# One written order for all five engines in a fused attention and hardswish kernel

## The chip, the cores and the metric

The kernel runs on one core of a Trainium2 chip. The core has five engines, each with its own in-order instruction queue. PE (TensorE) does matrix products from SBUF into PSUM, DVE (VectorE) and ACT (ScalarE) do elementwise work and read PSUM, POOL (GpSimd) does elementwise work in SBUF, and SP (SyncE) issues most DMA transfers. Engines meet through semaphores: an instruction that waits holds everything behind it on its own queue and nothing on the others. PSUM has eight banks of 128 x 512 float32 words. The metric is the time of one execution on the device in microseconds (us), lower is better; the median of several runs is compared.

## The reference

Eight batches (B) of eight heads (H), 512 local and 32 global tokens, head size 64, all float32. Global queries attend to all 544 keys, local queries to the 32 global keys and to local keys at a distance of at most 32. The heads are put side by side (512 columns) and go through an MLP of width 2048:

```python
s_g = scale * q_g @ concat(k_g, k_l).T          # 32 x 544
out_g = softmax(s_g) @ concat(v_g, v_l)
s_ll = where(abs(i - j) <= 32, scale * q_l @ k_l.T, -1e9)
a_l = softmax(concat(scale * q_l @ k_g.T, s_ll))
out_l = a_l @ concat(v_g, v_l)
x = concat(out_g, out_l)                        # (8*544) x 512
h = x @ w_in                                    # 512 -> 2048
out = (h * clip(h + 3, 0, 6) / 6) @ w_out       # 2048 -> 512
```

## The kernel before

**Units of work.** The 64 heads are taken as 32 pairs, numbered p = 0 to 31; pair p belongs to batch b = p // 4 and is its m = p % 4. For each pair:

- `load` (lines 113 to 125): SP brings k, q and v, 256 KB each, into staging buffers `stg` (13 of them); `cast` (127 to 136) makes them fp16 (`kn`, `qn`, and v into `vt`); `vshift` (138 to 141) copies half of `vt` to `vb`, which holds the values shifted by half a block; `vglob` (143 to 147) puts the global values there; `kglob` (198 to 201) puts the global keys between the local ones.
- `emit_T` (203 to 227) transposes keys and queries. Batches 0 and 1 do it on PE (four 128 x 128 transposes into PSUM, copied out by DVE or ACT); from batch 2 on SP issues one DMA transpose for each. `qwrap` (229 to 231) repeats 32 query columns.
- `emit_S` (233 to 255): the local scores in two halves (ch 0 and 1), for both heads, so 16 matmuls in all; ACT takes the exponential into `E`. The band is applied in one of two ways: either PE first adds a mask (`mneg`, two matmuls of 512 columns for each half, line 242), or DVE multiplies `E` by a 0/1 mask afterwards (`mk`, line 254, two for each half).
- `emit_SG` and `emit_PG` (257 to 314): scores and values of the global queries. `emit_AV` (275 to 299): values of the local queries, 32 matmuls, then DVE's reciprocal and product into `xn`. `emit_X` (316 to 331) transposes `xn` into `xt`, on PE for batches 0 and 1, by DMA from batch 2 on. `emit_XG` (333 to 342) normalises the global rows into `xg`.

The MLP of a batch (`moe_units`, 344 to 380) has a first product (16 column chunks c, each four matmuls over m from `xt`, line 354), ACT's ReLU (359), DVE's gate (361) into `gt`, and a second product (line 370: four output tiles t of 16 matmuls each, in groups of four, c4), whose result is copied out (374) and stored by SP (376). The first product of a batch needs the `xt` of all four of its pairs. After batch 7 the 256 global rows of all batches go through the same MLP as a ninth set (called 8 in the change), with 256 columns in the first product.

**Weights.** 16 + 16 loads of 256 KB (`load_w`) and as many casts (`cast_w`). Global keys and queries come in strips of 64 KB, one for each batch (`load_g`), and are transposed on PE in `emit_G`.

**PSUM.** Seven banks rotate in the pool `psp` (line 52), one tag for all tiles; the eighth holds the global values.

**What sets the order.** The program is written as calls of these functions; the framework's planner then orders each engine's instructions by priorities, dependencies and costs. Where `pin` (94 to 103) is called, it chains every instruction of the named engines to the one traced before it on that engine, without a semaphore, so that the planner keeps the traced order there. Line 608 pins all five engines (`ALL`) for the opening, from the loads to the scores of pair 7 and the first part of batch 1's MLP. For the loop over pairs (610 to 666), which mixes one pair's attention with 8 or so MLP units, and for the end, only SP and POOL (`QUEUES`) are pinned; PE, ACT and DVE are left to the planner. A call such as `emit_S` traces PE's, ACT's and DVE's parts together, and all of a batch's MLP comes in units of a chunk (first product) or of four matmuls (second product). Nearly all casts, shifts and global copies stand on POOL.

Of the kernel before, what the change touches and what calls it, by code (L numbers as in the profile page):

```python
# [14 lines left out]
def kernel(  # L15
# [90 lines left out]
    ALL = (ET.SP, ET.Pool, ET.PE, ET.Activation, ET.DVE)  # L106

    st = {}

    def stage():  # L110
        return wrk.tile([P, 512], FP32, tag="stg", name="stg", bufs=NSTG)

    def load(p, what="kqv"):
        b, m = divmod(p, NM)
        s = st.setdefault(p, {})
        for c in what:
            src = {"k": k_l, "q": q_l, "v": v_l}[c]
            t = stage()
            if c != "v" and b < NRUN:
                nc.sync.dma_start(out=t.rearrange("p (h x) -> p h x", h=2),  # L120
                                  in_=src[b, 2 * m:2 * m + 2].rearrange("h (p j) d -> p h (j d)", j=NT))
            else:
                nc.sync.dma_start(out=t.rearrange("p (h kb d) -> p (h kb) d", h=2, kb=NT),
                                  in_=src[b, 2 * m:2 * m + 2].rearrange("h (kb p) d -> p (h kb) d", p=P))
            s[c + "f"] = t.rearrange("p (h kb d) -> p kb h d", h=2, kb=NT)

    def cast(p, what, eng):
        b, m = divmod(p, NM)
        s = st[p]
        for c in what:  # L130
            if c == "v":
                o = vts[b % NV][:, :, 2 * m:2 * m + 2, 0:D]
            else:
                s[c + "n"] = wrk.tile([P, NT, P], FP16, tag=c + "n", name=c + "n", bufs=4)
                o = s[c + "n"].rearrange("p kb (h d) -> p kb h d", h=2)
            eng.tensor_copy(out=o, in_=s[c + "f"])  # L136
# [15 lines left out]
    w_st = {}  # L152

    def load_w(kind, i):
        t = stage()
        if kind == "in":
            qd, m = divmod(i, NM)
            nc.sync.dma_start(out=t, in_=moe_w_in[m * P:(m + 1) * P, qd * 512:(qd + 1) * 512])
# [43 lines left out]

    def emit_T(p, qdve=False):
        b, m = divmod(p, NM)
        s = st[p]
        kT = kTs[b % 2][:, m]
        kv = kT[:, 0:NT * KW].rearrange("p (u c) -> p u c", u=NT)
        qT = wrk.tile([P, Sl + W], FP16, tag="qT", name="qT", bufs=4)
        s["qT"], s["kT"] = qT, kT
        if b >= NRUN:  # L210
            for c, o in (("k", kv[:, :, 0:P]),
                         ("q", qT[:, W:Sl + W].rearrange("p (u c) -> p u c", u=NT))):
                nc.sync.dma_start_transpose(out=o, in_=s[c + "n"].rearrange("p kb c -> p (kb c)"))
            return
        ps = {}
        for c in "kq":
            ps[c] = ps_tile("psT" + c, FP16)[:, 0:Sl]
            for j in range(NT):
                nc.tensor.matmul(out=ps[c][:, j * P:(j + 1) * P], lhsT=s[c + "n"][:, j], rhs=ident,
                                 is_transpose=True)  # L220
        qcopy = nc.vector.tensor_copy if qdve else nc.scalar.copy
        nc.vector.tensor_copy(
            out=kv[:, :, 0:P].rearrange("p u (i j) -> p u i j", j=NT),
            in_=ps["k"].rearrange("p (j u i) -> p u i j", j=NT, u=NT))
        qcopy(out=qT[:, W:Sl + W].rearrange("p (i j) -> p i j", j=NT),
              in_=ps["q"].rearrange("p (j i) -> p i j", j=NT))
        nc.vector.tensor_copy(out=qT[:, 0:W], in_=qT[:, Sl:Sl + W])

    def qwrap(p):
        qT = st[p]["qT"]  # L230
        nc.gpsimd.tensor_copy(out=qT[:, 0:W], in_=qT[:, Sl:Sl + W])

    def emit_S(p, ch, pe_mask=False):
        s = st[p]
        qT, kT = s["qT"], s["kT"]
        if ch == 0:
            s["E"] = wrk.tile([P, 2, 2, Sl], FP16, tag="E", name="E", bufs=3)
        E = s["E"]
        pss = [ps_tile(f"psS{e}") for e in range(2)]
        if pe_mask:  # L240
            for e in range(2):
                nc.tensor.matmul(out=pss[e], lhsT=ident, rhs=mneg[:, ch], start=True, stop=False,  # L242
                                 skip_group_check=True)
        for w in range(NT):
            c0 = w * KW if ch == 0 else ((w - 1) % NT) * KW + D
            for e in range(2):
                r = slice(e * D, (e + 1) * D)
                nc.tensor.matmul(out=pss[e][:, w * P:(w + 1) * P], lhsT=kT[r, c0:c0 + P],  # L248
                                 rhs=qT[r, w * P:(w + 1) * P], start=not pe_mask, stop=True,
                                 skip_group_check=True)  # L250
        for e in range(2):
            nc.scalar.activation(out=E[:, ch, e], in_=pss[e], func=EXP, scale=qk_scale)  # L252
        for e in range(0 if pe_mask else 2):
            nc.vector.tensor_tensor(out=E[:, ch, e], in0=E[:, ch, e],  # L254
                                    in1=mk[:, ch].rearrange("p w c -> p (w c)"), op=mult)
# [19 lines left out]
    def emit_AV(p):  # L275
        b, m = divmod(p, NM)
        E = st[p]["E"]
        vt, vb = vts[b % NV], vbs[b % NV]
        xn = wrk.tile([P, NT, P], FP16, tag="xn", name="xn", bufs=3)
        st[p]["xn"] = xn  # L280
        for w2 in range(NT // 2):
            po = ps_tile("pav").rearrange("p (w c) -> p w c", w=2)
            for i in range(2):
                w = 2 * w2 + i
                for e in range(2):
                    h = 2 * m + e
                    o = po[:, i, e * DV:e * DV + D + 1]
                    nc.tensor.matmul(out=o, lhsT=E[:, 0, e, w * P:(w + 1) * P],  # L288
                                     rhs=vt[:, w, h, 0:D + 1], start=True, stop=False,
                                     skip_group_check=True)  # L290
                    nc.tensor.matmul(out=o, lhsT=E[:, 1, e, w * P:(w + 1) * P],  # L291
                                     rhs=vb[:, (w - 1) % NT, h, 0:D + 1], start=False, stop=True,
                                     skip_group_check=True)
            pv = po[:, :, 0:2 * DV].rearrange("p w (e c) -> p w e c", e=2)
            rc = wrk.tile([P, 2, 2, 1], FP32, tag="rc", name="rc", bufs=4)
# [223 lines left out]
    for c in range(HEAD, NC):  # L519
        u1(c)  # L520
# [182 lines left out]
```

## Time and profile before

| | us |
|---|---|
| median of 3 runs (328.93 to 331.13) | 329.35 |
| the profiled execution, own time | 329.07 |
| its span, first to last instruction | 327.2 |
| PE busy | 307.9 (94%) |
| DVE busy | 209.3 (64%) |
| ACT busy | 202.5 (62%) |
| POOL busy | 134.3 (41%) |

How to read the rows: the page gives each engine's busy time, then the span in 40 slices whose digit is the busy share in tenths. A group row has line, engine, operation, output and inputs, shapes and count; behind the first bar stand busy time in us and the mean ns of one instruction, behind the second the engine's idle time just before them and what ended it. Instructions overlap in the pipeline, so busy time divided by the count can be less than the mean. A row of the timeline starts with its start and its length in us. "SPq" is SP's queue: the length of an issue there includes what it waited for. PE's ends are modelled, so a busy PE is not always PE at full rate. In rows of DMA issues the last number is the median time from issue to landing.

### The profile page before, as it was taken

Reading aid. Unit: us, or ns where it says so; the run is one execution under the profiler, and the core shown is the slowest. Engines: PE = TensorE matmul, PEld = TensorE weight load, DVE = VectorE, ACT = ScalarE, POOL = GpSimd, SP = SyncE. Lnnn points to the kernel's source line nnn. Section 1 sums busy time; section 2 is a strip of 40 time slices with the busy share of each in tenths; the row PEclk is TensorE's granted clock in tenths of the full one; section 3 lists DMA queues with packets and bytes.
Section 4 is the critical chain, followed back from the end, with each engine's and each line's share of the span. In section 5 each row is a group of like instructions: output and inputs, shape, how many; then the busy total and the mean of one; then the engine's idle time right before and its main releaser. Section 6 shows DMA issues by size and latency. Waiting matters only on the chain.

```text
span 327.2 us, 7442 instructions
## 1 busy us (share of the span) xinstructions
PE 307.9 (94%) x2779; PEld 160.5 (49%) x2779; DVE 209.3 (64%) x469; ACT 202.5 (62%) x401; POOL 134.3 (41%) x240
## 2 busy tenths in 40 slices
PE   7799999999989489999999999999999999999994
PEld 2454446654545245545555455555555555444571
DVE  5377854669967379548955697469745874382260
ACT  8556866688825278448844785468646864481260
POOL 5879868708923834463436244535300000000000
PEclk9799999999999999999999999999999999999998
DMA  8999999999979997999979999799944012101202
GB/s 208 311 374 331 302 259 232 239 193 148 186 150 178 187 221 149 180 211 192 195 116 167 206 163 181 158 198 176 154 107 109 19 21 82 64 0 34 93 5 64
DMA packets 143011, 53.70 MB, mean 164 GB/s; under 512 B 130432, under 2 KB 134528, under 8 KB 142976
## 3 DMA queue, kind: packets, MB, share of 16 engines
q1 hardware_dynamic: 140800, 52.97, 77.8%
q0 software_dynamic: 2176, 0.26, 1.3%
q8 instruction: 22, 0.36, 0.5%
q14 instruction: 13, 0.11, 0.1%
HBM read 35.13 MB, written 8.91 MB: 135 GB/s over the span
## 4 chain that ended last, share of the span: by engine, by line
PE 78%; DVE 9%; DMA 5%; ACT 4%; issue 1%; SPq 1%; POOL 1%; DVEq 0%; ACTq 0%
PE psH L354 33%; PE po L370 31%; PE psS L248 4%; DMA xt<-xn 3%; DVE E L254 3%; ACT E L252 2%; PE pav L291 2%; PE pav L288 2%; DVE gt L361 2%; DMA stg<-in_v_l_dram 2%; PE pg L311 1%; PE psS L242 1%; PE psSG L265 1%; DVE xn L297 1%; ACT t L359 1%
## 5 line engine op out<-in xcount | busy, mean ns | idle before, releaser
L370 PE MATMUL po<-wout,gt 128*128 128x512 f16 x544 | 126.3, 379 | 0.0
L354 PE MATMUL psH<-xt,win 128*128 128x512 f16 x512 | 118.9, 379 | 6.5 <-DMA xt<-xn 5.6
L359 ACT ACTIVATE t<-psH,half_col 128x512 f32<-128x512 f32 (+1 forms) x144 | 91.0, 669 | 25.2 <-PE psH L354 20.0
L361 DVE SCALAR_TENSOR_TENSOR gt<-t,psH 128x512 f16<-128x512 f32 (+1 forms) x144 | 90.4, 653 | 25.2 <-ACT t L359 24.5
L252 ACT ACTIVATE E<-psS 128x512 f16<-128x512 f32 x128 | 66.6, 602 | 46.5 <-PE psS L248 46.4
L354 PEld LDWEIGHTS <-win 128*128 128x128 f16 x576 | 53.5, 98 | 56.0 <-issue 3.3
L370 PEld LDWEIGHTS <-gt 128*128 128x128 f16 x544 | 49.8, 98 | 54.4
L254 DVE TENSOR_TENSOR E<-E,mk 128x512 f16<-128x512 f16 x100 | 51.2, 540 | 9.2 <-ACT E L252 7.2
L136 POOL CAST kn<-stg 128x512 f16<-128x512 f32 x31 | 19.5, 630 | 45.2 <-DMA stg<-in_k_l_dram 44.2
L374 ACT COPY ot<-po 128x512 f32<-128x512 f32 x17 | 10.0, 588 | 36.6 <-PE po L370 36.6
L296 DVE RECIPROCAL rc<-pav 128x4 f32<-128x4 f32 x64 | 10.2, 172 | 29.8 <-PE pav L291 29.7
L374 DVE COPY ot<-po 128x512 f32<-128x512 f32 x17 | 11.7, 690 | 24.6 <-PE po L370 24.6
L297 DVE TENSOR_TENSOR xn<-pav,rc 128x256 f16<-128x256 f32 x64 | 26.2, 422 | 1.4
L136 POOL CAST vt<-stg 128x512 f16<-128x512 f32 x32 | 20.4, 638 | 15.6 <-DMA stg<-in_v_l_dram 13.0
L136 POOL CAST qn<-stg 128x512 f16<-128x512 f32 x32 | 20.8, 651 | 12.8 <-DMA stg<-in_q_l_dram 12.8
L248 PEld LDWEIGHTS <-kT 64*128 64x128 f16 x512 | 14.9, 94 | 18.4 <-issue 16.1
L248 PE MATMUL psS<-qT,kT 64*128 64x128 f16 x512 | 21.8, 219 | 0.7 <-ACT E L252 0.5
L288 PEld LDWEIGHTS <-E 128*128 128x128 f16 x256 | 17.8, 97 | 7.5 <-issue 4.1
L141 POOL COPY vb<-vt 64x512 f16<-64x512 f16 x32 | 20.3, 634 | 2.1
L291 PE MATMUL pav<-vb,E 128*128 128x65 f16 x256 | 20.1, 193 | 0.4 <-DVE E L254 0.3
L288 PE MATMUL pav<-vt,E 128*128 128x65 f16 x256 | 20.2, 192 | 0.1
L291 PEld LDWEIGHTS <-E 128*128 128x128 f16 x256 | 16.8, 97 | 3.9 <-DVE E L254 0.8
(74 smaller groups left out, 223.7 us busy)
## 6 DMA issues: line engine op xcount, KB each, us to landing
stg<-in_k_l_dram SPq DMA_DIRECT2D x32, 256.0 KB, 3.9
stg<-in_q_l_dram SPq DMA_DIRECT2D x32, 256.0 KB, 4.3
stg<-in_v_l_dram SPq DMA_DIRECT2D x32, 256.0 KB, 4.8
out_dram<-ot SPq DMA_DIRECT2D x24, 256.0 KB, 2.2
stg<-in_moe_w_in_dram SPq DMA_DIRECT2D x16, 256.0 KB, 6.3
stg<-in_moe_w_out_dram SPq DMA_DIRECT2D x16, 256.0 KB, 5.6
out_dram<-ot SPq DMA_DIRECT2D x8, 192.0 KB, 2.3
out_dram<-ot SPq DMA_DIRECT2D x16, 64.0 KB, 1.9
```

The costliest lines, as they stand in the source:

```text
L136: eng.tensor_copy(out=o, in_=s[c + "f"])
L248: nc.tensor.matmul(out=pss[e][:, w * P:(w + 1) * P], lhsT=kT[r, c0:c0 + P], rhs=qT[r, w * P:(w + 1) * P], start=not pe_mask, stop=True, sk ...
L252: nc.scalar.activation(out=E[:, ch, e], in_=pss[e], func=EXP, scale=qk_scale)
L254: nc.vector.tensor_tensor(out=E[:, ch, e], in0=E[:, ch, e], in1=mk[:, ch].rearrange("p w c -> p (w c)"), op=mult)
L288: nc.tensor.matmul(out=o, lhsT=E[:, 0, e, w * P:(w + 1) * P], rhs=vt[:, w, h, 0:D + 1], start=True, stop=False, skip_group_check=True)
L291: nc.tensor.matmul(out=o, lhsT=E[:, 1, e, w * P:(w + 1) * P], rhs=vb[:, (w - 1) % NT, h, 0:D + 1], start=False, stop=True, skip_group_chec ...
L297: nc.vector.tensor_tensor(out=xn[:, 2 * w2:2 * w2 + 2].rearrange("p w (e d) -> p w e d", e=2), in0=pv[:, :, :, 0:D], in1=rc.to_broadcast([ ...
L354: nc.tensor.matmul(out=ps[:, 0:n], lhsT=w_in_t[m][:, c * P:(c + 1) * P], rhs=rhs(m), start=(m == 0), stop=(m == NM - 1), skip_group_check= ...
L359: nc.scalar.activation(out=t1[:, 0:n], in_=ps[:, 0:n], func=RELU, bias=half_col, scale=1.0 / 6.0)
L361: nc.vector.scalar_tensor_tensor(out=gts[c][:, 0:n], in0=t1[:, 0:n], scalar=1.0, in1=ps[:, 0:n], op0=amin, op1=mult)
L370: nc.tensor.matmul(out=po[t][:, 0:dm], lhsT=gts[c][:, t * P:(t + 1) * P], rhs=w_out_t[c // 4][:, c % 4], start=(c == 0), stop=(c == NC - 1))
L374: (nc.scalar.copy if t % 2 else nc.vector.tensor_copy)(out=ot, in_=po[t][:, 0:dm])
```

## The change

Every function is cut into steps of a single engine, the whole program is written as one list of 2069 such steps, and all five engines are pinned to it from the first step to the last. Nothing is left to the planner. Each PSUM tile and each buffer of `stg`, `kn`, `qn`, `qT`, `E`, `xn`, `t1` and `ot` gets its place from a written list (`SEATS`) in place of a rotation; the numbers of places stay (7 in PSUM, 13 staging buffers, and so on).

With the list these things differ from before:

- **Masks.** 16 mask matmuls in place of 28 (pairs 0 to 3, without pair 0's second half, and pair 7's second half); 112 DVE multiplies in place of 100.
- **Transposes.** PE does 20 of the key and query transposes in place of 16 (also one each of pairs 8, 9, 10 and 12) and 9 output transposes in place of 8 (also pair 10); DMA does 44 and 23 in place of 48 and 24.
- **Engines of the copies.** Of 96 casts of k, q and v POOL has 55, DVE 25 and ACT 16; of 32 weight casts POOL 19, DVE 9, ACT 4; two of the five casts of the global strips are on DVE. 12 of the 32 value shifts, 14 of the 32 query wraps and 21 of 40 copies of global values are on DVE, 4 more on ACT. Of the 34 output copies ACT has 23.
- **Order.** The first product's chunks are taken in a free order and split over m, so that matmuls of several chunks alternate; loads, stores and transposes on SP have a free order too (some loads come many pairs ahead of their cast, some stores long after their copy).

The arithmetic is otherwise the same. In the list a step is a short name and its arguments: `Hp.2.0.0.1` is the first product of batch 2, chunk 0, m from 0 to 1; `Op.2.0.0` the second product of batch 2, tile 0, group 0; `Xd.11` pair 11's output transpose by DMA; `ca.3.k.v` the cast of pair 3's k on DVE (v DVE, a ACT, g POOL).

```diff
-    psp = ctx.enter_context(tc.tile_pool(name="psp", bufs=7, space=bass.MemoryType.PSUM))
+    psp = ctx.enter_context(tc.tile_pool(name="psp", bufs=1, space=bass.MemoryType.PSUM))
+    SEATS = """
+ps 01234560123455401054036254631405623160243524341624132540134236503651631653106451034561204513240513015320465
...
+stg 0123456789abc0145362798b0a1c53647289a0b1c356489a27b103c645892a7b103c6589247bac03592681ba47053268cb17403529
...
+xn 01201201201202102101201210210210 ;
...
+"""
+    seat = {tag: iter("".join(s)) for tag, *s in (line.split() for line in SEATS.split(";"))}
+
     def ps_tile(name, dtype=FP32):
-        return psp.tile([P, 2048 // (4 if dtype == FP32 else 2)], dtype, tag="ps", name=name)
+        return psp.tile([P, 2048 // (4 if dtype == FP32 else 2)], dtype, tag="ps" + next(seat["ps"]),
+                        name=name)
+
+    def buf(tag, shape, dtype, name):
+        return wrk.tile(shape, dtype, tag=tag + next(seat[tag]), name=name, bufs=1)
...
+    ENG = {"v": nc.vector, "g": nc.gpsimd, "a": nc.scalar}
+
+    def copy(eng, out, in_):
+        (nc.scalar.copy if eng == "a" else ENG[eng].tensor_copy)(out=out, in_=in_)
...
+    def cast(p, c, eng):
         b, m = divmod(p, NM)
+        if c == "v":
+            o = vts[b % NV][:, :, 2 * m:2 * m + 2, 0:D]
+        else:
+            st[p, c + "n"] = buf(c + "n", [P, NT, P], FP16, c + "n")
+            o = st[p, c + "n"].rearrange("p kb (h d) -> p kb h d", h=2)
+        copy(eng, o, st[p, c + "f"])
...
+    def T_dma(p, c):
+        o = (kT_of(p)[:, 0:NT * KW].rearrange("p (u c) -> p u c", u=NT)[:, :, 0:P] if c == "k"
+             else qT_of(p)[:, W:Sl + W].rearrange("p (u c) -> p u c", u=NT))
+        nc.sync.dma_start_transpose(out=o, in_=st[p, c + "n"].rearrange("p kb c -> p (kb c)"))
...
+    def S_mask(p, ch):
+        st[p, ch] = [ps_tile(f"psS{e}") for e in range(2)]
+        for e in range(2):
+            nc.tensor.matmul(out=st[p, ch][e], lhsT=ident, rhs=mneg[:, ch], start=True, stop=False,
+                             skip_group_check=True)
...
+    def X_dma(p):
+        nc.sync.dma_start_transpose(out=xt_of(p).rearrange("p (w c) -> p w c", w=NT),
+                                    in_=st[p, "xn"].rearrange("p w c -> p (w c)"))
...
+    def H_pe(f, c, m0, m1):
+        if m0 == 0:
+            st["H", f, c] = ps_tile("psH")
+        for m in range(m0, m1):
+            x = xg[:, m].rearrange("p b s -> p (b s)") if f == B else xts[f, m]
+            nc.tensor.matmul(out=st["H", f, c][:, 0:FN(f)], lhsT=w_in_t[m][:, c * P:(c + 1) * P],
+                             rhs=x, start=(m == 0), stop=(m == NM - 1), skip_group_check=True)
+
+    def H_act(f, c):
+        st["t", f, c] = t1 = buf("t1", [P, Sl], FP32, "t1")
+        nc.scalar.activation(out=t1[:, 0:FN(f)], in_=st["H", f, c][:, 0:FN(f)], func=RELU,
+                             bias=half_col, scale=1.0 / 6.0)
...
+    def O_pe(f, t, c4):
+        if c4 == 0:
+            st["O", f, t] = ps_tile("po")
+        for c in range(4 * c4, 4 * c4 + 4):
+            nc.tensor.matmul(out=st["O", f, t][:, 0:dm], lhsT=gts[f, c][:, t * P:(t + 1) * P],
+                             rhs=w_out_t[c // 4][:, c % 4], start=(c == 0), stop=(c == NC - 1))
...
+    TOKENS = {
+        "ld": load, "ca": cast, "vs": vshift, "vg": vglob, "vG": vglobs, "lv": load_vg,
+        "lw": load_w, "cw": cast_w, "lg": load_g, "Gc": G_cast, "Gp": G_pe, "Ge": G_ev,
+        "kg": kglob, "Td": T_dma, "Tp": T_pe, "Te": T_ev, "qw": qwrap, "Sm": S_mask, "Sp": S_pe,
+        "Se": S_exp, "Sv": S_mul, "Qp": SG_pe, "Qe": SG_exp, "Ap": AV_pe, "An": AV_norm,
+        "Pp": PG_pe, "Xd": X_dma, "Xp": X_pe, "Xe": X_ev, "Ga": XG_act, "Gv": XG_dve,
+        "Hp": H_pe, "Ha": H_act, "Hv": H_dve, "Op": O_pe, "Oe": O_ev, "Os": O_st,
...
+    def run(tokens):
+        for tok in tokens:
+            name, *args = tok.split(".")
+            TOKENS[name](*[int(a) if a.isdigit() else a for a in args])
+
+    ORDER = """
+id ld.1.q iv wm.7 ld.1.k fg.1.v ld.0.q fv.0.v ld.2.q lg.k.0 fv.1.v ld.0.k ca.1.q.g ld.3.k lv.0 Tp.1.q ov.1.0
+ld.2.k ca.1.k.g Te.1.q.a ld.3.q ig ov.0.0 Tp.1.k qw.1.v ld.0.v ov.0.1 lw.i.7 im Gc.k.0.g ov.0.2 ld.1.v
...
+Op.1.1.2 Oe.1.3.v Se.12.0.1 Se.12.0.0 vs.10.v ld.14.k Pp.8 An.9.1 Pp.9 Ap.11.1 Sv.12.0.1 Xd.9 Ap.11.0 An.11.1
+Pp.10 Ap.10.0 Op.1.2.0 An.11.0 An.10.0 ld.12.v Op.1.2.1 Sv.12.0.0 Xd.11 Ap.10.1 Sp.12.1 An.10.1 Sp.13.0
+ld.23.k Op.1.2.2 Gc.k.4.v Se.13.0.1 ld.15.k Gc.q.4.v Se.13.0.0 Sv.13.0.1 ld.19.q Gp.k.4 Se.12.1.0 Op.1.2.3
+ld.13.v Se.12.1.1 Sv.12.1.0 Os.1.3 Qp.12 Hp.2.0.0.1 Ge.k.4.v Xp.10 Qe.12 Hp.2.1.0.2 Xe.10.v vg.3.2.a
...
+Ap.13.0 Os.1.2 Hv.2.13 ca.15.v.g Op.2.0.0 Td.16.k An.13.0 vs.15.g Ap.13.1 Hp.2.8.2.3 ca.17.k.g Hp.2.8.3.4
...
+"""
+
+    run(ORDER.split())
     pin(*ALL)
-
-    for p in range(2 * NM - 1, NPAIR):
...
-        pin(*QUEUES)
...
-    pin(*QUEUES)
```

More of the change, by code (lines that the diff above doesn't have):

```diff
@@ L106, with load @@
     ALL = (ET.SP, ET.Pool, ET.PE, ET.Activation, ET.DVE)
+    ENG = {"v": nc.vector, "g": nc.gpsimd, "a": nc.scalar}
+    def copy(eng, out, in_):
+        (nc.scalar.copy if eng == "a" else ENG[eng].tensor_copy)(out=out, in_=in_)
     st = {}
     def stage():
-        return wrk.tile([P, 512], FP32, tag="stg", name="stg", bufs=NSTG)
-    def load(p, what="kqv"):
+        return buf("stg", [P, 512], FP32, "stg")
+    def load(p, c):
         b, m = divmod(p, NM)
[L115 to L125, printed above, removed]
@@ L204, in emit_T, with kT_of @@
+    def kT_of(p):
         b, m = divmod(p, NM)
[L205 to L243, printed above, removed]
+        return kTs[b % 2][:, m]
@@ new lines, in qwrap, with S_pe @@
+    def qwrap(p, eng):
+        qT = qT_of(p)
+        copy(eng, qT[:, 0:W], qT[:, Sl:Sl + W])
+    def S_mask(p, ch):
[3 more added lines that the diff above has]
+                             skip_group_check=True)
+    def S_pe(p, ch):
+        added = (p, ch) in st
+        if not added:
+            st[p, ch] = [ps_tile(f"psS{e}") for e in range(2)]
+        kT, qT = kT_of(p), qT_of(p)
@@ L273, with AV_pe @@
     pgs = {}
-    def emit_AV(p):
+    def AV_pe(p, w2):
         b, m = divmod(p, NM)
-        E = st[p]["E"]
+        E = st[p, "E"]
         vt, vb = vts[b % NV], vbs[b % NV]
[L279 to L295, printed above, removed]
-            nc.vector.reciprocal(out=rc, in_=pv[:, :, :, D:D + 1])
-            nc.vector.tensor_tensor(
-                out=xn[:, 2 * w2:2 * w2 + 2].rearrange("p w (e d) -> p w e d", e=2),
-                in0=pv[:, :, :, 0:D], in1=rc.to_broadcast([P, 2, 2, D]), op=mult)
@@ L304, in emit_PG @@
         vt = vts[b % NV]
[L305 removed]
+        if b not in pgs:
             pgs[b] = psg.tile([P, NM, 2, Sg], FP32, tag="pg", name="pg")
@@ L430 @@
[L430 to L444 removed]
+    FILL = -30000.0
@@ new lines, with init_v, init_g @@
+    mv = mneg.rearrange("p c (w q) -> p c w q", w=NT)
+    def init_v():
+        nc.vector.memset(wz, 0.0)
+        nc.vector.memset(ones, 1.0)
+        nc.vector.memset(mb, 0.0)
+        nc.vector.memset(mb[D + Sg:P, 1], FILL)
+        nc.vector.memset(half_col, 0.5)
+    def init_g():
+        for rows, ch, base, step, mulp in ((slice(0, P), 0, 0, 1, -1), (slice(0, P), 0, 2 * W, -1, 1),
+                                           (slice(0, D), 1, 0, -1, 1)):
+            nc.gpsimd.affine_select(out=mb[rows, ch], in_=mb[rows, ch], compare_op=is_ge, fill=FILL,
+                                    base=base, pattern=[[step, P]], channel_multiplier=mulp)
@@ L453, in warm @@
             nc.tensor.matmul(out=ps, lhsT=wz[:, 0:P], rhs=wz, skip_group_check=True)
-    def vglob_act(b):
-        for u in range(NT):
-            nc.scalar.copy(out=vbs[b % NV][rg, u, :, 0:D], in_=vg[rg, b])
-    warm(7)
-    fill_v(0, nc.vector)
-    ones_v(0)
-    nc.scalar.memzero(qgz)
-    cast(0, "k", nc.vector)
-    mv = mneg.rearrange("p c (w q) -> p c w q", w=NT)
-    nc.vector.tensor_copy(out=mv, in_=mb.unsqueeze(2).to_broadcast([P, 2, NT, P]))
-    nc.vector.memset(mv[:, 0, 0, 0:W], fill)
```

693 lines of the change are left out of this document (339 added, 354 removed).

## Prediction

> **What bounds the kernel now.** I read the page's totals and slices first, then busy time by stretches of 16.36 us, then the chain of waits.
>
> ```profile
> PE 307.9 (94%) x2779; PEld 160.5 (49%) x2779; DVE 209.3 (64%) x469; ACT 202.5 (62%) x401; POOL 134.3 (41%) x240
> PE   7799999999989489999999999999999999999994
> ```
>
> ```profile
> 0.00:16.36 16.36, 12.04 (x103) 5.68 (x104) 7.34 (x26) 11.78 (x20) 11.77 (x26) 0.90 1.02 260
> ...
> 81.80:98.16 16.36, 15.13 (x160) 8.04 (x158) 13.77 (x30) 9.36 (x21) 9.95 (x18) 1.00 0.93 168
> 98.16:114.52 16.36, 12.17 (x130) 6.54 (x129) 8.37 (x20) 6.62 (x17) 9.93 (x18) 1.00 0.99 182
> 114.52:130.88 16.36, 15.20 (x138) 7.95 (x138) 13.52 (x28) 13.33 (x25) 6.67 (x14) 1.00 0.92 185
> ...
> 147.24:163.60 16.36, 16.36 (x151) 8.34 (x147) 14.23 (x30) 14.10 (x27) 6.71 (x13) 1.00 1.19 194
> ```
>
> After the range the columns are the stretch, busy time of PE, its weight loads, DVE, ACT and POOL, then granted clock and DMA. PE is the bound, but two things are seen. From about 131 us PE is full, and no order makes it fuller; only the start and the stretch at 98 to 131 us hold real idle. And where PE is full, DVE reaches 14.23 of 16.36 us (87%): with the interleaving of before, that is the highest share I can show beside a full PE.
>
> ```profile
> 164.62 2.60 PE po L370 x12
> ...
> 173.07 2.60 PE po L370 x12
> ...
> 281.10 13.81 PE psH L354 x64
> ...
> 308.72 6.99 PE psH L354 x64
> ...
> 322.65 0.59 ACT ot L374
> ```
>
> These are pieces of the chain in order of time: start, length, what. 64 matmuls of 512 columns take 13.81 us, so 0.2158 us each. One head pair's beat is 173.07 - 164.62 = 8.45 us and holds 32 such matmuls (6.91 us), so a pair's attention matmuls take 1.54 us. PE's last matmul ends at 322.65; the profiled execution took 329.07 us (the median of the runs shown is 329.35), so 6.42 us lie outside PE's work. The tail keeps its form (copy, then stores), so I keep 6.42.
>
> **Where the two orders meet.** I cut the written list right after step Op.2.0.0. Behind it stand 323 + 412 = 735 matmuls of 512 columns (158.6 us), the global rows' first product (6.99 us) and, by counting scores and value steps, 18.5 pairs of attention (28.5 us): 194.1 us of PE work, none of it transposes or masks. Before reaches the point with 194.1 us left at 322.65 - 194.1 = 128.6 us. So the time after is T + 194.1 + 6.42 + new stalls, where T is when the new order reaches that cut; T = 128.6 would be no change.
>
> **PE's own list up to the cut.**
>
> ```profile
> L242 PE MATMUL psS<-mneg,ident 128*128 128x512 f16 x28 | 9.1, 409 | 0.0
> ...
> L219 PE MATMUL psTk<-ident,kn 128*128 128x128 f16 x32 | 3.6, 242 | 2.5 <-POOL kn L136 2.5
> ```
>
> Removed: 28 mask matmuls become 16. At 0.2158 (warm) to 9.1/28 = 0.325 us (with the cold start) the 12 gone are worth 2.6 to 3.9 us. Added: key or query transposes on PE rise from 16 to 20 and output transposes from 8 to 9, so 5 x 4 matmuls at up to 3.6/32 = 0.1125 us, at most 2.3 us. Net gain 0.3 to 3 us. The list to the cut is 189 + 132 = 321 matmuls (69.3), 13.5 pairs (20.8), 16 masks (3.5) and 29 groups of four transposes at 0.45 (13.1, an upper price): 106.7 us. T cannot be much below that.
>
> **DVE's list up to the cut.**
>
> ```profile
> L361 DVE SCALAR_TENSOR_TENSOR gt<-t,psH 128x512 f16<-128x512 f32 x128 | 83.7, 682 | 21.2 <-ACT t L359 20.8
> L254 DVE TENSOR_TENSOR E<-E,mk 128x512 f16<-128x512 f16 x100 | 51.2, 540 | 9.2 <-ACT E L252 7.2
> L297 DVE TENSOR_TENSOR xn<-pav,rc 128x256 f16<-128x256 f32 x64 | 26.2, 422 | 1.4
> ...
> L296 DVE RECIPROCAL rc<-pav 128x4 f32<-128x4 f32 x64 | 10.2, 172 | 29.8 <-PE pav L291 29.7
> ...
> L222 DVE COPY kT<-psTk 128x512 f16<-128x512 f16 x8 | 5.5, 687 | 5.8 <-PE psTk L219 5.8
> ...
> L522 DVE COPY vgs<-vg 32x512 f16<-32x512 f16 x2 | 0.5, 281 | 0.0
> ...
> L136 DVE CAST kn<-stg 128x512 f16<-128x512 f32 x1 | 0.5, 452 | 0.2 <-DMA stg<-in_k_l_dram 0.2
> ```
>
> The removed masks come back here: 100 multiplies become 112. Casts come too: of 96 + 32 + 5 casts, 36 stand on DVE and 20 on ACT, where before had nearly all on POOL. To the cut DVE has 45 gates at 83.7/128 = 0.654 (29.4), 40 multiplies at 0.512 (20.5), 26 normalisations at 0.422 + 0.172 less their overlap, (26.2 + 10.2)/64 = 0.569 (14.8), 27 casts at 0.452 (12.2), 23 copies out of PSUM between 0.281 and 0.687, taken at 0.55 (12.6), 28 small copies and products at 0.281 (7.9), and the fills, about 6 (an estimate: they sit in the 7.34 us of the first stretch). Together 103.4 us. In before DVE is busy for about 89 us of the first 130.88 (eight such stretches, of which the first and the last stand above). So the change makes DVE as long as PE in this part: 103 beside at most 107. Neither can be full while each waits for the other. I take DVE at 90%, between the 87% seen beside a full PE and 100%: T = 103.4/0.90 = 114.9, a gain of 13.7 us. At 87% T is 118.9, at 95% 108.8.
>
> [...]
>
> ```profile
> L254 DVE TENSOR_TENSOR E<-E,mk 128x512 f16<-128x512 f16 x30 | 17.6, 628 | 4.7 <-ACT E L252 4.5
> ```
>
> ```profile
> L254 DVE TENSOR_TENSOR E<-E,mk 128x512 f16<-128x512 f16 x8 | 3.3, 424 | 0.6 <-ACT E L252 0.3
> ```
>
> The same multiply took 628 ns in 60 to 131 us, with POOL at work, and 424 ns in 262 to 290 us, where POOL had nothing. Forty of them are 17.0 to 25.1 us instead of 20.5, so DVE's list is 99.9 to 108.0. [...]
>
> **The transfers.** The wait with a name on PE is this, with the beat of the SP queue behind it:
>
> ```profile
> PE psH L354 <- DMA xt<-xn: 5.6, 4, 2.5
> ```
>
> ```profile
> 10.12 12.39 SPq L158 DMA_DIRECT2D stg<-in_moe_w_in_dram  x16
> ```
>
> ```profile
> 99.68 0.42 SPq L123 DMA_DIRECT2D stg<-in_k_l_dram  x1
> 100.14 0.76 SPq L123 DMA_DIRECT2D stg<-in_q_l_dram  x1
> 100.95 1.33 SPq L123 DMA_DIRECT2D stg<-in_v_l_dram  x1
> ...
> 105.71 1.22 SPq L322 DMA_TRANSPOSE xt<-xn  x1
> 107.02 0.54 SPq L376 DMA_DIRECT2D out_dram<-ot  x1
> ...
> 113.16 1.20 SPq L322 DMA_TRANSPOSE xt<-xn  x1
> ```
>
> Pair 11's output transpose, the last that batch 2's first product needs, is issued at 113.16 us. In the new list the queue issues ahead of it 44 loads at 2.51/3 = 0.84 (36.8), 32 weight loads at 12.39/16 = 0.77 (24.8), 16 strips (6.7 at 0.42), 10 transposes at 1.22 (12.2) and 4 stores (2.2): 82.7 us, with 0.05 between issues 88. Before had queued 51 loads, 14 + 3 transposes and the stores of two batches there. PE's list up to batch 2 is 252 matmuls, 12 pairs, masks and transposes, 89 us; at the pace of T it is there at 96. So the queue's floor leaves room of some 6 us beside a landing of 2.5, and the 5.6 us wait can go. It returns in small: in ten of the 23 cases less than 6 us of PE work stand between an output transpose and its first reader, against
>
> ```profile
> stg<-in_k_l_dram SPq DMA_DIRECT2D x32, 256.0 KB, 3.9
> ...
> stg<-in_v_l_dram SPq DMA_DIRECT2D x32, 256.0 KB, 4.8
> ...
> stg<-in_moe_w_out_dram SPq DMA_DIRECT2D x16, 256.0 KB, 5.6
> ...
> kT<-kn SPq DMA_TRANSPOSE x24, 4.2
> ...
> xt<-xn SPq DMA_TRANSPOSE x24, 2.5
> ```
>
> 2.5 us of landing plus the normalisation before it. Key and query transposes have at least 5.7 us against 4.2. I put 3 us for new stalls (0.3 us at each of ten places), bounds 0 and 6. Seats replace a rotation by a fixed buffer for each tile; they cost nothing where the earlier reader is done, and what they cost otherwise is in these 3.
>
> Sum: 114.9 + 194.1 + 6.42 + 3 = 318.4. With the ends (99.9/0.95 but no less than PE's 106.7, no stall; 108.0/0.87, 6 us of stalls) 307 to 331; most of it between 311 and 325.
>
> **Rivals.** (1) Loads met too early. A cast on DVE or ACT that waits for its load holds the gates, exponentials and evictions queued behind it, and PE behind those once the seven PSUM seats are full. 22 of the 54 casts of q, k, v and weights there have under 6.5 us of PE work between load and cast, against landings of 3.9 to 5.6 and the queue's own delay. For it: the waits for loads stood on POOL before, which PE seldom needs soon. Against it: nearly all 22 still have more than the landing. If each costs 0.8 us, 17.6 us go: 318.4 - 3 + 17.6 = 333. The gain is used up at 13.7/22 = 0.6 us each.
>
> (2) DVE and POOL hold each other up in casts and copies too, as the multiply does in the rows above.
>
> ```profile
> L136 POOL CAST kn<-stg 128x512 f16<-128x512 f32 x31 | 19.5, 630 | 45.2 <-DMA stg<-in_k_l_dram 44.2
> ```
>
> POOL's new list to the cut is some 70 such steps and a few small ones, about 50 of 115 us. If 50 casts and copies on DVE each wait half a POOL step, 0.3 us, in the 43% of the time in which POOL is at work, that is 6.5 us: T = 109.9/0.90 = 122.1, time 325.6. [...]
>
> (3) The queue decides after all. Its transposes wait in order for casts on three engines, its loads for seats, its stores for evictions. Beyond the 6 us of room each microsecond of waiting moves batch 2. With 20 us of it pair 11 lands at 88 + 20 + 2.5 = 110.5, the 17.7 us of PE's list from there to the cut end at 128, and the time is 329. Against it: before's own list ahead of 113.16, at the same prices, is 51 loads, weights, strips, 17 transposes and some nine stores, about 106, so it waited for 7.
>
> (4) The engines do not keep the written order, or the planner had nearly this one: only PE's shorter list is left, 326 to 329.
>
> **How the numbers follow.** Forecast 0.62 (of it 0.07 below 311), rival 1 0.18, rival 2 0.10, rival 3 0.08, rival 4 0.02. I take the forecast's 318.4. Measurements of this kernel can tell about 1% from no change, so faster is below 326.1, slower above 332.6. Faster: 0.61 + 0.06 of rival 2 + 0.04 of rival 3 = 0.71. Slower: more than half of rival 1, and a few hundredths where it and rival 2 or 3 meet, 0.15. Same: the rest, 0.14. Leaving out 0.07 below 311 and 0.12 above 331, the range is 311 to 331; the forecast's own is 311 to 325.
>
> **What would show it.** Right: PE's idle between 98 and 131 us nearly gone, DVE near 90% in the first 115 us, the wait on xt below 3 us, batch 2's first product before 100 us, mask matmuls x16. Wrong: DVE or ACT idle behind stg transfers, PE idle behind DVE's casts, POOL casts or DVE casts well above the rows here, or new PE gaps after 131 us, where before has none.

## The result, and the profile after

The changed kernel takes 320.92 us (median of four runs, 320.04 to 321.71) against 329.14 for before in the same comparison: a ratio of 0.974, with a 95% interval of 0.969 to 0.980. The prediction was 318.4, in 311 to 331, and "faster". The profiled execution took 320.04 us, its span 318.3.

The totals and slices of the changed kernel's page, and two groups that speak of the prediction's prices:

```profile
PE 306.1 (96%) x2787; PEld 161.6 (51%) x2787; DVE 222.1 (70%) x538; ACT 217.6 (68%) x434; POOL 86.8 (27%) x155
PE   5889999999999999999998999999999999999994
...
L300 DVE TENSOR_TENSOR E<-E,mk 128x512 f16<-128x512 f16 x112 | 49.2, 469 | 15.3 <-ACT E L296 14.9
...
L133 POOL CAST kn<-stg 128x512 f16<-128x512 f32 x15 | 10.4, 694 | 27.5 <-DMA stg<-in_k_l_dram 25.1
```

The dip of before's row between 90 and 123 us (8, 9, 4, 8) is gone: from the fourth slice to the last but one PE's row is 9 with a single 8. The span is 8.9 us shorter and PE's busy time only 1.8 us (306.1 beside 307.9), so 7.1 us of the gain are idle time. The same by stretches (columns as in the prediction):

```profile
0.00:16.36 16.36, 11.36 (x83) 5.69 (x83) 8.91 (x28) 9.31 (x17) 10.50 (x25) 0.90 0.93 260
16.36:32.72 16.36, 15.60 (x167) 8.46 (x167) 12.99 (x38) 14.44 (x28) 9.40 (x15) 1.00 1.05 311
32.72:49.08 16.36, 16.26 (x137) 8.30 (x135) 14.62 (x30) 12.08 (x25) 10.51 (x17) 1.00 1.03 303
49.08:65.44 16.36, 16.05 (x234) 10.33 (x233) 13.51 (x38) 14.41 (x34) 10.16 (x17) 1.00 0.79 174
65.44:81.80 16.36, 16.36 (x159) 8.56 (x157) 14.54 (x30) 14.99 (x30) 4.55 (x11) 1.00 0.85 178
81.80:98.16 16.36, 16.36 (x204) 9.15 (x202) 15.62 (x44) 8.77 (x19) 3.95 (x8) 1.00 1.00 192
98.16:114.52 16.36, 16.36 (x120) 8.21 (x118) 14.34 (x33) 14.47 (x28) 3.17 (x6) 1.00 1.06 218
...
163.60:179.96 16.36, 15.16 (x144) 7.85 (x142) 8.54 (x21) 12.00 (x28) 6.73 (x12) 1.00 0.96 209
```

From 32.72 to 114.52 PE is busy for 81.4 of 81.8 us, where before had 74.4; beside it DVE reaches 15.62 of 16.36 us. The opening is as long as it was. Pair 11's output transpose now leaves the queue at 96.89 us, not at 113.16:

```profile
94.95 1.22 SPq L372 DMA_TRANSPOSE xt<-xn  x1
...
96.89 1.22 SPq L372 DMA_TRANSPOSE xt<-xn  x1
```

and of PE's own waits these are the two longest in total (a third, 1.2 us at the very start, is in before too), the first in the opening, the second at 170 us:

```profile
PE psGT L213 <- POOL kgn L133: 2.1, 1, 2.1
PE psH L408 <- DMA xt<-xn: 1.2, 1, 1.2
```

The chain of waits ends as before, with the last copy just after PE's last matmul:

```profile
302.79 11.24 PE po L426 x52
314.05 0.59 ACT ot L133
```

PE has done 321 matmuls of 512 columns, as many as the list has up to the cut, at about 116.4 us (312 by 114 us, 327 by 118); the same count is used for T in the runs below. That leaves 314.05 - 116.4 = 197.6 us for work that I put at 194.1, and 320.04 - 314.05 = 6.0 outside PE's work.

### The profile page after: what moved, and what is told of

Read it like the earlier page. It is cut to its first block, busy times and chain, and to the rows that moved or that the text cites. A ratio compares the mean times of both kernels' runs of the same rounds, so it can differ in the third digit from the quotient of the medians.

```text
span 318.3 us, 7431 instructions
## 1 busy us (share of the span) xinstructions
PE 306.1 (96%) x2787; PEld 161.6 (51%) x2787; DVE 222.1 (70%) x538; ACT 217.6 (68%) x434; POOL 86.8 (27%) x155
## 4 chain that ended last, share of the span: by engine, by line
PE 84%; DVE 8%; DMA 3%; ACT 1%; issue 1%; SPq 1%; POOL 1%; DVEq 0%
PE psH L408 35%; PE po L426 34%; PE psS L286 5%; PE pav L333 2%; PE pav L336 2%; DVE E L300 2%; PE pg L360 2%; DMA xt<-xn 2%; DMA stg<-in_k_g_dram 1%; DVE xn L346 1%; PE psSG L310 1%; ACT E L296 1%; PE psS L274 1%; DVE gt L419 1%; PE psTq L248 1%
## 5 line engine op out<-in xcount | busy, mean ns | idle before, releaser
L426 PE MATMUL po<-wout,gt 128*128 128x512 f16 x544 | 131.7, 379 | 0.1
L408 PE MATMUL psH<-xt,win 128*128 128x512 f16 x512 | 125.2, 379 | 1.4 <-DMA xt<-xn 1.2
L133 ACT COPY ot<-po 128x512 f32<-128x512 f32 x23 | 13.3, 589 | 21.7 <-PE po L426 18.4
L333 PE MATMUL pav<-vt,E 128*128 128x65 f16 x256 | 22.9, 193 | 0.6 <-DVE qT L133 0.3
L336 PE MATMUL pav<-vb,E 128*128 128x65 f16 x256 | 22.9, 193 | 0.2
L133 POOL CAST qn<-stg 128x512 f16<-128x512 f32 x20 | 13.0, 651 | 24.7 <-DMA stg<-in_q_l_dram 24.4
L133 POOL CAST vt<-stg 128x512 f16<-128x512 f32 x20 | 12.9, 643 | 24.9 <-DMA stg<-in_v_l_dram 20.1
L133 POOL COPY vb<-vt 64x512 f16<-64x512 f16 x20 | 12.7, 640 | 23.0 <-DVE vt L133 17.6
L133 POOL CAST kn<-stg 128x512 f16<-128x512 f32 x15 | 10.4, 694 | 27.5 <-DMA stg<-in_k_l_dram 25.1
L314 ACT ACTIVATE Eg<-psSG 128x256 f16<-128x256 f32 x32 | 12.6, 392 | 5.3 <-PE psSG L310 3.3
```

Of the source, the lines that this page charges most:

```text
L133: (nc.scalar.copy if eng == "a" else ENG[eng].tensor_copy)(out=out, in_=in_)
L408: nc.tensor.matmul(out=st["H", f, c][:, 0:FN(f)], lhsT=w_in_t[m][:, c * P:(c + 1) * P], rhs=x, start=(m == 0), stop=(m == NM - 1), skip_gr ...
L426: nc.tensor.matmul(out=st["O", f, t][:, 0:dm], lhsT=gts[f, c][:, t * P:(t + 1) * P], rhs=w_out_t[c // 4][:, c % 4], start=(c == 0), stop=( ...
```

## Experiments

Each is the changed kernel with one edit, unless it says otherwise.

**The planner orders PE, ACT and DVE.** The list, its seats and its engines stay; only SP and POOL are held to it.

```diff
     run(ORDER.split())
-    pin(*ALL)
+    pin(*QUEUES)
```

> The written list is traced as it is, with its seats, engines, masks and transposes, but only SP and POOL are held to it; the planner orders PE, ACT and DVE, as it does in the kernel before. Theory (the written order of the three compute engines carries the gain, since it keeps PE fed where the planner's order did not): most of the 8 us goes, 325 to 332 us, with new idle of PE ahead of the cut. Rival (the lists of SP and POOL, the shared copies and the shorter mask list carry it): 319 to 323.

Measured: 340.45 us, ratio to before 1.033 (1.026 to 1.039); 8 us worse than the theory's upper end. The written order of the three compute engines is worth about 20 us beside these lists of SP and POOL and these seats. (The seats were written for the list's own order; the planner's order with rotating seats was not run.) The stretch from 65 to 82 us in this kernel:

```profile
65.44:81.80 16.36, 14.54 (x151) 7.75 (x149) 14.71 (x39) 13.88 (x31) 6.71 (x13) 1.00 0.85 176
```

There is no one hole; one or two microseconds go in most stretches up to 270 us, with PE behind DVE's gates (2.6 us for scores, 2.2 for the second product).

**Before, with all engines held to its own traced order.**

```diff
-        pin(*QUEUES)
+        pin(*ALL)
...
-    pin(*QUEUES)
+    pin(*ALL)
```

> The kernel before, with PE, ACT and DVE held to its own traced order in the loop over pairs as well. Theory (what counts is which order is written, not that one is): a pair's scores, exponentials and values are traced close together, so PE waits for ACT and DVE inside each pair; 24 pairs at 0.5 to 1.5 us, so 340 to 365 us. Rival (holding the engines to a written order is itself the gain): 326 or less.

Measured: 335.95 us, ratio 1.020 (1.014 to 1.025). A written order is no gain in itself. But the loss is 7 us, not 11 to 36, and it isn't made of 24 small waits; most of it stands at the start of batch 2's first product, where PE is busy for 3.7 us less than in before and its granted clock is 0.86, where before had 1.00 (another 3.0 us are four waits of the global queries' values for `xg`):

```profile
98.16:114.52 16.36, 8.50 (x81) 4.30 (x80) 4.63 (x12) 4.37 (x12) 8.59 (x16) 0.86 1.12 184
```

```profile
PE psH L354 <- DMA xt<-xn: 8.2, 3, 6.8
```

Held to its order, PE can't take other work while pair 11's output lands; the planner had put some there (the 12.17 us that before has in this stretch).

**Seats by rotation.**

```diff
-psp = ctx.enter_context(tc.tile_pool(name="psp", bufs=1, ...
+psp = ctx.enter_context(tc.tile_pool(name="psp", bufs=7, ...
-        return psp.tile(..., tag="ps" + next(seat["ps"]), name=name)
+        return psp.tile(..., tag="ps", name=name)
-        return wrk.tile(shape, dtype, tag=tag + next(seat[tag]), name=name, bufs=1)
+        n = {"stg": 13, "E": 3, "xn": 3}.get(tag, 4)
+        return wrk.tile(shape, dtype, tag=tag, name=name, bufs=n)
```

> Seats by rotation again, 7 in PSUM and as many of each staging buffer as before; the order stays. Theory (with chunks taken in a free order tiles are freed out of turn, so a rotation makes PE wait for a seat whose reader is late): 323 to 330. Rival (seats do nothing): 320 to 322.

Measured: 321.48 us, ratio 0.975 (0.969 to 0.980), that of the changed kernel. With this order, the places written down do nothing that can be measured.

**Copies back on POOL.**

```diff
+        if n in ("ca", "cw", "vs", "vg", "vG") or n == "qw" and int(a[0]) >= 8:
+            a[-1] = "g"
```

> All casts of q, k, v and weights, the value shifts, the copies of global values and the later query wraps go back to POOL at their places in the list. Some 52 steps of 0.62 us move to POOL ahead of the cut, 32 us, so POOL has about 83 of 116 us there, and DVE loses about 17 us, ACT some 6. Theory (PE is the bound from about 33 us on, and POOL's chain only in the opening): the opening gets longer, 322 to 328. Rival (DVE's length ahead of the cut sets T): T falls by 8 or more, 309 to 315.

Measured: 325.3 us, ratio 0.987 (0.982 to 0.992): sharing the copies is worth about 4.4 us. DVE's shorter list gains nothing, against the rival. The place isn't the theory's, though. The first two stretches are as they were, and the loss comes after them, where POOL has 13 of 16.36 us, and once more at 164 us:

```profile
32.72:49.08 16.36, 14.96 (x114) 7.37 (x112) 10.29 (x23) 10.80 (x22) 12.92 (x22) 1.00 0.99 298
49.08:65.44 16.36, 14.57 (x214) 9.13 (x211) 8.25 (x25) 11.57 (x26) 13.06 (x25) 1.00 0.70 167
...
163.60:179.96 16.36, 13.34 (x125) 7.02 (x124) 4.89 (x13) 8.61 (x20) 4.86 (x8) 1.00 0.96 207
```

```profile
PE psH L408 <- DMA xt<-xn: 3.0, 1, 3.0
PE pav L336 <- POOL vb L133: 2.1, 3, 0.7
...
PE po L426 <- POOL wout L133: 1.6, 3, 1.1
```

PE now waits for the shifted values (2.1 us) and the weights' casts (1.6 us) themselves, and 3.0 us for an xt where the changed kernel's longest such wait is 1.2.

**Mask multiplies ahead of the cut, twice and not at all.**

```diff
+    for tok in steps[:cut]:
+        first += [tok] * (2 if tok.startswith("Sv.") else 1)
```

```diff
+    run([tok for tok in steps[:cut] if not tok.startswith("Sv.")] + steps[cut:])
```

> Each of the 40 mask multiplies ahead of the cut is done twice (the mask is 0 or 1, so the second changes nothing). DVE gets 19 to 25 us more there, at 0.47 to 0.63 each: its 96 us become 115 to 121, beside a T of 116. Theory (DVE has slack ahead of the cut, PE is the bound): DVE only now becomes the bound, T 120 to 128, time 324 to 332. Rival (DVE at 82% is already as full as the coupling of the two allows): T = 118/0.82 = 144, time 345 to 350.

> The 40 mask multiplies ahead of the cut are left out, so the band mask of those pairs is not applied where PE does not add it. DVE has 19 to 25 us less there. Theory (PE is the bound): 319 to 321, no change or 1 us from shorter chains. Rival (DVE's list sets T, as my prediction had it): T falls by 10 or more, 306 to 312.

Measured: twice 339.49 us (ratio 1.031, 1.027 to 1.035), not at all 321.19 (0.975, 0.970 to 0.980). Without the multiplies DVE has the work of

```profile
49.08:65.44 16.36, 16.36 (x237) 10.76 (x236) 9.53 (x30) 14.63 (x35) 10.05 (x18) 1.00 0.88 191
...
81.80:98.16 16.36, 16.36 (x203) 9.18 (x200) 10.27 (x30) 9.22 (x20) 3.10 (x7) 1.00 0.88 189
```

9.5 and 10.3 us in stretches where the changed kernel has 13.5 and 15.6, and PE is as full and the time the same (T is 115.7 us): DVE's length does not set T. Doubled, the time lies between the two theories. The 18.6 us more are about the whole of what was added:

```profile
65.44:81.80 16.36, 15.14 (x148) 9.17 (x145) 12.75 (x32) 9.02 (x20) 6.35 (x13) 0.71 0.92 157
```

```profile
PE pav L333 <- DVE E L300: 5.5, 4, 3.1
PE pav L336 <- DVE E L300: 3.1, 3, 1.4
```

PE waits 8.6 us for E, and its clock falls (0.71 in that stretch). In the profiled execution (341.17 us, the slowest of the four) the cut is reached at 138.0 us and DVE is busy for 115.4 of it: 84%, as in the changed kernel (83%). So DVE did not set T, but it had no slack for this work either. The second multiply also lengthens the chain from each exponential to its value product; whether that chain or DVE's load costs the time was not taken apart.

**Masks back on PE.**

```diff
+        if n in ("Sp", "Sv") and (int(a[0]), int(a[1])) in halves:
+            if n == "Sv":
+                continue
+            steps.append(f"Sm.{a[0]}.{a[1]}")
```

> The twelve mask matmuls that the change took from PE are put back, and their twelve multiplies leave DVE. Theory (PE is the bound): PE's list is 12 x 0.216 = 2.6 us longer, time 322.5 to 324.5. Rival (DVE's list sets T): DVE has 6 us less, time 314 to 319.

Measured: 321.46 us, ratio 0.975 (0.973 to 0.978), 0.5 us over the changed kernel and within what these runs can tell. Neither theory, by the time. The trace shows more: PE is full from 32.72 us to the cut and reaches it at 118.2 us instead of 116.4, so most of the 2.6 us are there, as the theory has it; behind the cut some of it is made up. The rival's gain did not come.

**The five transposes back to DMA, all, the output alone, the four others alone.**

```diff
+        if n in ("Tp", "Xp", "Te", "Xe") and int(a[0]) >= 8:
+            if n[1] == "p":
+                steps += ["skip", ".".join([n[0] + "d", *a])]
+            continue
```

(Each DMA transpose stands where the PE transpose stood. `skip` takes the PSUM seat that the transpose would have had. The two others test for `Xp`, `Xe` or for `Tp`, `Te` alone.)

> The key and query transposes of pairs 8, 9, 10 and 12 and the output transpose of pair 10, which the change does on PE, go back to DMA transposes at the same places in the list; their copies out of PSUM go. Theory (PE is the bound and the queue has room there): PE has 20 x 0.06 to 0.11 = 1.2 to 2.2 us less, and pair 10's output lands 2.5 us after its normalisation, with about that much PE work to its reader: 318 to 321. Rival (the queue is the second bound there, five more issues at 1.2 us): 324 to 328, with a wait on xt.

> Only pair 10's output transpose goes back to DMA, at its place in the list; the four key and query transposes stay on PE. All five back cost 8 us, with 4.7 us of PE idle ahead of batch 2's first product, 2.1 us on a kT and a clock of 0.90 to 0.92 around them. Theory (the landing of pair 10's output is what the list leaves no PE work for): 5 of the 8 us, 324 to 327. Rival (the queue was late from the four other transposes ahead of it): 320 to 322.

> Only the four key and query transposes of pairs 8, 9, 10 and 12 go back to DMA; pair 10's output stays on PE. Theory (the landing of pair 10's output is the large part): 2 to 3 us, from the wait on kT, 322 to 324. Rival (the queue is late from these four): 325 to 329.

Measured: all five 329.01 us (ratio 1.000, 0.997 to 1.003), pair 10's output alone 326.5 (0.990, 0.984 to 0.996), the four others 323.83 (0.981, 0.975 to 0.987). All five together cost 8.1 us, the whole gain; alone they cost 5.6 and 2.9, which add up to about that. The first run's theory fails; its rival has the wait on xt, but the time is 1 us over its range, and five issues at 1.2 us are not the cause, since pair 10's output alone costs 5.6. The later runs' theories have the split. In the kernel with all five back:

```profile
65.44:81.80 16.36, 14.24 (x134) 7.02 (x133) 13.88 (x27) 13.87 (x27) 4.74 (x9) 0.98 1.07 189
81.80:98.16 16.36, 16.36 (x182) 8.69 (x181) 12.93 (x36) 8.42 (x18) 4.28 (x9) 0.92 0.90 175
98.16:114.52 16.36, 11.66 (x88) 5.65 (x87) 7.86 (x21) 7.04 (x15) 2.50 (x4) 0.90 1.01 217
```

```profile
PE psH L408 <- DMA xt<-xn: 5.5, 2, 4.7
PE psSG L310 <- DMA kT<-kn: 2.1, 1, 2.1
```

Twice PE stands, 4.7 and 2.1 us, and behind both the granted clock is below 1. But the longer one is not the landing alone. Pair 10's last normalisation ends at about 100.1 us (an estimate: its last value matmul starts at 99.29 and takes 0.19 us, the reciprocal and the product behind it 0.18 and 0.42); on the queue four loads and a store stand between pair 11's output transpose, at 99.60, and pair 10's, at 104.97:

```profile
99.60 1.22 SPq L372 DMA_TRANSPOSE xt<-xn  x1
100.86 1.21 SPq L148 DMA_DIRECT2D stg<-in_k_l_dram  x2
102.11 0.76 SPq L148 DMA_DIRECT2D stg<-in_q_l_dram  x1
102.92 0.98 SPq L148 DMA_DIRECT2D stg<-in_v_l_dram  x1
103.95 0.92 SPq L442 DMA_DIRECT2D out_dram<-ot  x1
104.97 1.21 SPq L372 DMA_TRANSPOSE xt<-xn  x1
```

```profile
108.23 1.74 PE L408 MATMUL psH<-xt,win 128*128 128x512 f16 x4 [4.70 <-DMA xt<-xn]
```

From its issue to the matmul that waited for it 3.3 us pass. An estimate from these rows: issued at 100.8, right behind pair 11's, it would have landed at about 104.1, half a microsecond after PE ran out of other work (103.5). So these runs price a DMA transpose at the place of the PE transpose, not the best list with DMA transposes; a list with pair 10's ahead of the loads was not run. In 2 us steps, with pair 10's output alone back:

```profile
102.00:104.00 2.00, 0.00 (x0) 0.00 (x0) 0.00 (x0) 0.00 (x0) 0.00 (x0) 1.00 1.04 273
104.00:106.00 2.00, 0.34 (x1) 0.11 (x1) 0.00 (x0) 0.00 (x0) 0.00 (x0) 0.91 0.72 164
106.00:108.00 2.00, 2.00 (x13) 0.65 (x11) 0.58 (x1) 1.13 (x2) 0.00 (x0) 0.50 0.84 192
108.00:110.00 2.00, 2.00 (x14) 0.97 (x13) 1.40 (x4) 1.71 (x5) 1.43 (x3) 0.73 1.29 261
```

PE, DVE, ACT and POOL all stand idle for 2 us; then PE's clock reads 0.91, 0.50 and 0.73. The clock lost in these three rows, (0.09 + 0.50 + 0.27) x 2 us, is 1.7 us.

**One part alone: the five transposes on PE in the kernel before.**

```diff
+                if (p, c) in ((8, "q"), (9, "k"), (10, "k"), (12, "q")):
+                    pt = ps_tile("psT" + c, FP16)[:, 0:Sl]
+                    for j in range(NT):
+                        nc.tensor.matmul(out=pt[:, j * P:(j + 1) * P], lhsT=s[c + "n"][:, j], rhs=ident,
+                                         is_transpose=True)
+                    (nc.scalar.copy if c == "k" else nc.vector.tensor_copy)(
+                        out=o, in_=pt.rearrange("p (u c) -> p u c", u=NT))
+                    continue
...
-        if b >= NRUN:
+        if b >= NRUN and p != 10:
```

> One part alone: the kernel before, with the five transposes that the change moves to PE (queries of 8 and 12, keys of 9 and 10, output of 10) done on PE, everything else as it was. Theory (the five are needed by the written order, which has no room for their landing, and are no gain in themselves): 327 to 331, since before's wait of 4.9 us on xt ahead of 131 us is for pair 11 as much as for pair 10. Rival (taking five issues off the queue is the gain): its wait on xt goes, 321 to 325.

Measured: 325.98 us, ratio 0.989 (0.983 to 0.996), about 3.6 us. Between the two: the five are a gain in themselves, and less than half of the whole. (The planner is free here, so its order around the five may differ too.) Of the 5.6 us that PE waits for xt in before 1.0 is left, and a new wait comes in front of a query transpose:

```profile
81.80:98.16 16.36, 13.54 (x149) 7.30 (x148) 12.14 (x29) 7.26 (x17) 9.79 (x19) 1.00 0.80 154
98.16:114.52 16.36, 15.68 (x151) 8.11 (x150) 9.78 (x25) 9.69 (x23) 8.92 (x16) 1.00 1.00 208
```

```profile
PE psTq L216 <- POOL qn L136: 1.4, 1, 1.4
...
PE psH L362 <- DMA xt<-xn: 1.0, 1, 1.0
```

PE has 15.68 us at 98 to 114 where before had 12.17, and 13.54 just ahead of it where before had 15.13.

**Two places of the list rewritten.** Pair 1's first half of scores ahead of the global keys, and batch 4's two matmuls on pair 19's output behind five others (a fill and the PSUM seats of the opening move with them, not shown):

```diff
-Te.1.k.v Gp.k.0 ov.0.3 ca.0.k.g ... Tp.2.q Sm.1.0 Te.2.q.a
+Te.1.k.v Sm.1.0 Sp.1.0 Gp.k.0 ov.0.3 Se.1.0.0 Se.1.0.1 ca.0.k.g ... Tp.2.q Te.2.q.a kg.0.v
...
-ca.24.k.a Hp.4.13.2.4 Hp.4.4.0.1 Qe.20 Hp.4.4.1.2 Hp.4.8.3.4 Hp.4.3.1.2 Td.22.k ca.22.v.g Hp.4.4.2.3 Ha.4.8
-Hp.4.4.3.4 Hp.4.1.2.3 lv.6 Hp.4.1.3.4
+ca.24.k.a Hp.4.13.2.3 Hp.4.4.0.1 Qe.20 Hp.4.4.1.2 Hp.4.3.1.2 Td.22.k ca.22.v.g Hp.4.4.2.3 Hp.4.1.2.3 Hp.4.8.3.4 Ha.4.8
+Hp.4.4.3.4 lv.6 Hp.4.13.3.4 Hp.4.1.3.4
```

> The changed kernel with two places of its list rewritten. In the opening pair 1's first half of scores is done before the global keys (which it does not need), its exponentials follow at once, and the global keys' copy and a fill move up on DVE: PE waits 2.1 us for the cast of the global keys there. In batch 4's first product the two matmuls on pair 19's output come after five others that need it not: PE waits 1.2 us for that landing at 170 us. Theory (PE is the bound, so each idle microsecond taken out is one off the time, if no other wait follows it): 318 to 320. Rival (the opening is paced by the loads of v and by their casts, not by PE): the first part is worth nothing, 319.5 to 321.

Measured: 321.07 us (six runs, 319.21 to 323.28), ratio 0.974 (0.968 to 0.980): no better than the changed kernel. The two waits are gone or small:

```profile
PE psS L274 <- DVE mneg L465: 1.1, 1, 1.1
PE psH L408 <- DMA xt<-xn: 0.6, 2, 0.3
```

but another has come in the opening, and neither the 2 us of PE's idle there, as the rival had it, nor the 1.2 us at 170 us bought anything that six runs can show. Whether it is the loads of v or their casts that pace the opening was not taken apart.

## Why the prediction was right, and where it was not

**The sum.** T was put at 114.9 us and came out at about 116.4; what comes behind it beyond the 194.1 us of work at 3 us, all of it stalls, and came out at 3.5 (197.6 less 194.1), of which 1.7 us are idle time of PE and 1.8 us work above its prices; what lies outside PE's work at 6.42 and was 6.0. 116.4 + 197.6 + 6.0 is the 320.0 of the profile. The profiled execution is 1.6 us and the median 2.5 us over the forecast's 318.4.

**What the steps said.** The gain lies ahead of the cut and PE's hole at 98 to 131 us is closed: right. The opening stays as it was: PE is still idle for 5.0 and 0.8 us in the first two stretches. The wait on xt falls to 1.2 us (below 3 was said), pair 11's output transpose leaves at 96.89 us where the queue's floor was put at 88, and batch 2's first product starts at about 99.5, just before the 100 named. Mask matmuls are 16.

**The step that failed** is "Neither can be full while each waits for the other. I take DVE at 90%". DVE's rows up to the cut sum to 104.6 us, close to the 103.4 of the prediction. But DVE is busy for only 96.4 us, since an instruction often starts before the one ahead of it has ended (a product of 0.42 us starts at 85.61 us, the cast behind it at 85.95), and a sum of rows counts the overlap twice. So DVE was at 83% of T and not at 90%, and T did not come from it: with the 40 multiplies left out T is 115.7 us, and in one stretch DVE is at 95% beside a full PE.

What sets T is PE's own list with the opening, for which the prediction's 106.7 us had no term. PE is busy for 110.2 us up to the cut, 4.2 of them with eleven matmuls on a tile of zeros (`psW`) in the opening, which compute nothing of the result; it is idle for 5.8 us in the first 32.72 us and for 0.4 us from there to the cut. That 103.4/0.90 came within 1.5 us of the measured T is luck: too much DVE time over too high a share stood in for the opening. With the multiplies left out the same rule gives no more than PE's 106.7 and a time of 310, 11 us too little. With the multiplies doubled it gives (103.4 + 20.5)/0.90 = 137.7, and 138.0 was measured; there PE does wait for DVE.

**The transposes** were a term of cost only, "at most 2.3 us" of PE; what they save was put to the order of the queue. The runs show them as what this order rests on: with DMA transposes at the same places the gain is gone, pair 10's output landing 4.7 to 5 us after PE wants it, mostly because it is issued behind four loads and a store. In before's own order the five give 3.6 us.

**Rivals.** Loads met too early: PE has no wait for a cast on DVE or ACT above 0.3 us, so the waits are covered. POOL and DVE holding each other up: POOL's k casts take 694 ns in place of 630, and the five w_out casts on DVE 807 where 452 was the price of a cast (its nine k casts took 423); the multiply takes 488 ns at 60 to 116 us, with POOL at work, and 417 at 262 to 290, where POOL has nothing. That the one waits for the other no run shows; the 0.3 us for each step was an estimate. T hardly falls when DVE has 16 us less to do, and the time of 325.6 did not come. The queue as the limit did not hold for the changed kernel; the runs with transposes put back show what a late place in it costs. That the order is not kept or was there already is excluded by the kernel with the planner's order, 340.45 us.

**What stays open.** The parts don't add up to the whole in one way: copies back on POOL cost 4.4, the five transposes 8.1, the planner's order 20, each from the changed kernel; from the side of before only the transposes were tried, 3.6 us. How much the order alone gives before, with its own engines and transposes, was not run, nor a list rewritten for DMA transposes. That the opening is paced by something other than PE is argued from the last experiment, not shown.

## What to carry to other kernels

When one engine is at 94%, look for the stretch in which it isn't, and ask which transfer or chain it waits for there; here a handful of transposes moved from the DMA queue to the full engine paid, because they took a queue and a landing off the path. An order written out for all engines has little play on the chains that the full engine waits for: 40 multiplies more cost 18.6 us, one transpose moved to the queue 5.6, while work taken off DVE gave nothing back. A busy share of another engine is no bound; take work away from that engine before you believe it is one, and add some before you believe that it has slack. And don't add up rows to an engine's length where its instructions overlap.

## What the runs showed of the hardware

Behind some of its stands PE's clock fell. With the four key and query transposes back, PE waits 2.69 us for a kT, and then the clock reads 0.68, 0.50 and 0.96:

```profile
80.00:82.00 2.00, 0.00 (x0) 0.00 (x0) 1.69 (x3) 0.66 (x2) 0.36 (x2) 1.00 0.35 72
82.00:84.00 2.00, 1.67 (x16) 0.87 (x17) 0.00 (x0) 0.86 (x2) 0.51 (x1) 0.68 0.73 183
84.00:86.00 2.00, 2.00 (x11) 0.89 (x10) 0.76 (x2) 0.23 (x1) 0.27 (x2) 0.50 0.46 101
86.00:88.00 2.00, 2.00 (x18) 0.96 (x16) 0.44 (x1) 1.15 (x3) 1.21 (x3) 0.96 1.00 224
```

The clock lost in these rows, (0.32 + 0.50 + 0.04) x 2 us, is 1.7 us, as in the kernel with pair 10's output alone back; here the stand cost this on top of its length. The length of the stand does not decide it in these runs. With all five back 2.12 us without a matmul, up to 80.37 us, were enough: the four matmuls of 512 columns that start at 80.95 took 1.79 us and four at 83.25 took 1.64, where four at 85.62 took 1.03. In before two waits of 2.54 and 2.35 us, up to 108.89 and 115.68 us, left the clock at 1.00, and so did the 3.0 us that the kernel with its copies back on POOL waits for an xt (1.00 in its stretch from 163.60 to 179.96 us). What decides it was not shown.
